# Attention followed by two gated layers on one core: later slots for three weights' conversions, the softmax epsilon on ScalarE, four buffers for P

## The chip, the core and the metric

One core of a Trainium2 chip. The metric is device time of the kernel in microseconds (us), as the median of three executions. One further execution was profiled. Its trace gives every instruction's engine, start and duration, and all rows below come from it. Engines: PE is TensorE, DVE is VectorE, ACT is ScalarE, POOL is GpSimd, and SP issues the transfers.

## The reference

Only the structure matters here. All weights come as 64-bit floats and everything is computed in 32 bits.

```python
scores = q @ k.T / 8 + (cum[:, None] - cum[None, :])   # 4 x 8 heads, 576 positions, causal
attn = np.exp(scores - np.max(scores, axis=-1, keepdims=True))
attn = attn / (np.sum(attn, axis=-1, keepdims=True) + 1e-09)
x = attn @ v                                            # -> 2304 x 512
h = x @ w_in                                            # 512 -> 2048
x = (h * np.tanh(softplus(h))) @ w_out                  # 2048 -> 512
out = (((x @ w1) * (x @ w2)) @ w3) @ wo2                # 512 -> 1024 -> 1024 -> 512
```

## The kernel before

The program has two phases. The second is a long run of matmuls for the two gated layers (lines 889, 908 and 928) that read converted weights. The first holds the attention and everything that prepares the second.

**Attention.** Heads are taken in 16 pairs, each pair in nine units (four row blocks per head and one block for the remaining 64 rows of both), so there are 144 units. A unit u goes through `scores` on PE (lines 391, 392, 401) into one of two PSUM tiles `ps_s`; `softmax_a` on DVE (lines 415 to 418), which writes the masked scores into the buffer `P[u % 3]` and finds their extreme, followed by an exponential on ACT (line 419) in place; `transposes` on PE (line 455) from P into one of two PSUM tiles `ps_t`; and `pt_parts`, which takes the transposed block out of `ps_t` as a high part on ACT (line 483) and a low part on DVE (line 485). After a head's units, `pv` multiplies by V (line 503). The row sums of a pair are finished by `inv_sums` (lines 426 and 427, 128x9 values), transposed (line 434), written to memory and read back as a broadcast tile R (lines 437 to 444); `x_rows` (515, 516) and `x_parts` (521, 88, 102) then make the pair's rows of x.

**What fills PE.** Between the units PE runs matmuls that have no hurry: the products of w3 and wo2 (line 550), and from batch to batch the first gated layer's `x @ w_in` (line 580), 12 matmuls to a tile, whose results go to memory through line 587 and 588. These need x of the four pairs of one batch, all of them for every tile: the last three of the 12 need the batch's last pair.

**Conversions.** A 64-bit weight block is loaded by SP (line 111, two buffers), scaled by POOL for the keys u (w_out) and v (w1 and w2) (line 124, two halves) or by ACT for the others (line 126), completed by three DVE instructions (lines 134, 135, 136, two output buffers), and for u and v stored by SP (line 143). There are 32 such jobs u0 to u15 and v0 to v15.

**What sets the order.** `phase_a` writes the code slot by slot: a table puts job i of the 32 at slot `W_OUT_SLOT + int(W_OUT_STEP * i)`. The code's order gives each instruction a priority. The build's scheduler then picks, from the instructions whose inputs and buffers it takes to be free, the one that comes first, so that an instruction written late can still stand early on its engine. The order that results is fixed in the program; at run time each engine takes its instructions strictly in that order, and a waiting one holds up all behind it.

Of the kernel before, what the change touches and what calls it, by code (L numbers as in the profile page):

```python
# [8 lines left out]
F32 = mybir.dt.float32  # L9
# [3 lines left out]
AF = mybir.ActivationFunctionType  # L13
ALU = mybir.AluOpType
# [4 lines left out]
B, H, S, D = 4, 8, 576, 64  # L19
# [24 lines left out]
MID = 7  # L44
EARLY = 10
W3_STEP = 2.25
W_OUT_STEP = 2.25
PRE = 6
WP_END = 51
W_IN_SLOT = 34  # L50
W_IN_STEP = 1.25
W_OUT_SLOT = 62
L1_S = (42, 75, 114, 153)

MM_PAIRS = ((0, 0), (0, 1), (1, 0))
# [12 lines left out]
class Kernel:  # L68
# [116 lines left out]
    def att_pool(self):  # L185
        nc = self.nc
        self.attp = self.tc.tile_pool(name="att", bufs=1)
        a = self.att = self.attp.__enter__()
        self.psp = self.tc.tile_pool(name="psa", bufs=1, space=PSUM)
        p = self.psp.__enter__()  # L190
        self.ps_s = [p.tile([128, 512], F32, name=f"ps_s{i}") for i in range(2)]
        self.ps_t = [p.tile([128, 512], F32, name=f"ps_t{i}") for i in range(2)]
        self.ps_v = p.tile([128, 1024], F32, name="ps_v")
        self.ident = a.tile([128, 128], F32, name="ident")
        self.m1 = a.tile([128, 512], BF16, name="m1")
        self.m4 = a.tile([128, TB], BF16, name="m4")
        self.pt = a.tile([128, 6 * PT_N + 3 * 64], F32R, name="pt")
        self.pt4 = self.pt[:, 6 * PT_N:]
        self.TT = [a.tile([128, 2, 1216], F32R, name=f"T{i}") for i in range(3)]
        self.T = [(t[:, 0], t[:, 1]) for t in self.TT]  # L200
        self.P = [a.tile([128, n], F32, name=f"P{i}") for i, n in enumerate((512, 512, S))]


    def decay_log(self):
# [67 lines left out]
    def zeros(self):  # L272

        nc = self.nc
        z = self.m1[:, :384]
        nc.gpsimd.memset(self.P[2][0:4], 1.0)
        for i in (0, 2, 1):
# [8 lines left out]
            for c in (d0, d0 + S):  # L286
                nc.scalar.copy(t2[0:4, c:c + S], self.P[2][0:4])

# [115 lines left out]
    def softmax_a(self, u):  # L404
        _, _, c = self.unit(u)
        nc = self.nc
        n = S if c == 4 else 128 * (c + 1)
        P = self.P[u % 3]
        i = (0, 1, 2, 3, 5, 6, 7, 8, 4)[u % 9]
        if u % 9 == 0:  # L410
            self.sums = self.att.tile([128, 16], F32, name=f"sum{u // 9}", tag="sum", bufs=2)
        st = self.sums[:, 9 + u % 3:10 + u % 3]
        ttr = nc.vector.tensor_tensor_reduce
        if c < 4:
            ttr(P[:, :n], self.ps_s[u % 9 % 2][:, :n], self.m1[:, 512 - n:], -0.125, 3.0e38, ALU.add, ALU.min, st)  # L415
        else:
            ttr(P[:, :TB], self.ps_s[0][:, :TB], self.m1[:, :TB], -0.125, 3.0e38, ALU.add, ALU.min, self.sums[:, 12:13])
            ttr(P[:, TB:n], self.ps_s[1][:, :TB], self.m4, -0.125, self.sums[:, 12:13], ALU.add, ALU.min, st)
        nc.scalar.activation(P[:, :n], P[:, :n], AF.Exp, bias=st, scale=-1.0,  # L419
                             accum_out=self.sums[:, i:i + 1])  # L420

    def inv_sums(self):

        nc = self.nc
        r = self.sums[:, 0:9]
        nc.vector.tensor_scalar(r, r, 1e-9, None, ALU.add)
        nc.vector.reciprocal(r, r)
        self.inv = r

# [18 lines left out]

    def transposes(self, u):
        _, _, c = self.unit(u)  # L450
        P = self.P[u % 3]
        for kc in range(c + 1):
            o = 128 * (kc % 4)
            k = 64 if kc == 4 else 128
            self.nc.tensor.transpose(self.t_bank(u, kc)[0:k, o:o + 128], P[:, 128 * kc:128 * kc + k], self.ident)  # L455
# [190 lines left out]
    def phase_a(self):  # L646
# [48 lines left out]
        def job(s, key, src, fin, *a):  # L695
            at(s, self.cv_load, key, src)
            conv.setdefault(s + 1, []).append(key)
            at(s + 2, fin, *a)
# [7 lines left out]
        for i in range(32):  # L706
# [3 lines left out]
            else:  # L710
                key, src, dst = f"v{f}", self.cols((self.w1, self.w2)[f % 2], f // 2), self.w12_scr
            job(W_OUT_SLOT + int(W_OUT_STEP * i), key, src, self.cv_store, key, dst[f])
        for p in range(NPAIR):
# [329 lines left out]
```

## Time and profile before

| what | value |
|---|---|
| median of three executions | 1089.82 us (1088.87 to 1092.64) |
| profiled execution | 1095.71 us |
| its span, from the first instruction to the last | 1094.0 us |
| PE busy | 980.8 us (90%) |
| DVE, ACT, POOL busy | 788.5, 639.1, 592.7 us |
| mean granted PE clock | 0.954 |

Busy time counts an instruction from start to end, also at a lower clock. The granted clock is told as a share of 2.4 GHz, so that 0.50 is the lower level, 1.2 GHz. The profiled execution's own time is 1.71 us over its span and 5.89 us over the median.

### The profile page before, as it was taken

The page shows a single profiled execution, that of the slowest core. Times are in us where ns is not written, and L with a number is a line of the kernel's source. Part 1 is how long each engine was busy: PE and PEld are TensorE (multiplying, and loading weights), DVE is VectorE, ACT ScalarE, POOL GpSimd, SP SyncE. Part 2 cuts the span into 40 slices and gives each one's busy share as a digit, 9 for nine tenths or more (in the row PEclk, how much of TensorE's full clock was granted, in tenths as well). Part 3 has the DMA queues.
Part 4 walks back from the last instruction along what each step waited for, and adds up shares of the span by engine and source line. Part 5 has one row for each costly group of instructions (what it writes and reads, how often), then busy time and mean ns, then how long its engine had stood idle before and what let it go on. Part 6 is the DMA issues. An engine that isn't in the chain of part 4 may idle for free. (4 is left out here: it accounts for less than half of the span.)

```text
span 1094.0 us, 20534 instructions
## 1 busy us (share of the span) xinstructions
PE 980.8 (90%) x6784; PEld 935.2 (85%) x6784; DVE 788.5 (72%) x1800; ACT 639.1 (58%) x1660; POOL 592.7 (54%) x690
## 2 busy tenths in 40 slices
PE   0797778888789888998979999999999999999998
PEld 0576657788789878998878999999999999999998
DVE  7977788785666776643897886868868687886821
ACT  7676778876665677764666454545545454454511
POOL 5956677775666677623685453534545353453500
PEclk9898869899889998998999999999999999999999
DMA  7865457667667867425864111121111112111100
GB/s 212 207 209 173 131 164 219 195 183 222 199 201 229 249 203 219 150 72 170 298 188 126 39 44 45 44 61 39 50 45 44 50 44 61 39 50 40 27 23 22
DMA packets 107086, 136.37 MB, mean 125 GB/s; under 512 B 11092, under 2 KB 83172, under 8 KB 106980
## 3 DMA queue, kind: packets, MB, share of 16 engines
q1 hardware_dynamic: 106980, 135.07, 41.7%
q8 instruction: 53, 0.87, 0.3%
q14 instruction: 53, 0.43, 0.1%
HBM read 98.39 MB, written 36.54 MB: 123 GB/s over the span
## 5 line engine op out<-in xcount | busy, mean ns | idle before, releaser
L580 PE MATMUL ps_l<-x,wi 128*128 128x288 f32 x1536 | 250.6, 312 | 14.5 <-ACT x L88 4.1
L580 PEld LDWEIGHTS ps_l<-x,wi 128*128 128x128 f32 x1536 | 224.7, 198 | 20.5 <-ACT hst L587 5.2
L889 PE MATMUL ps_x<-g,wo 128*128 128x288 f32 x1536 | 224.5, 297 | 6.8 <-POOL g L102 3.7
L889 PEld LDWEIGHTS ps_x<-g,wo 128*128 128x128 f32 x1536 | 209.6, 189 | 11.0 <-POOL g L102 6.0
L102 POOL TENSOR_TENSOR g<-mb,g 128x288 fp32r<-128x288 f32 x128 | 111.5, 871 | 135.5 <-ACT g L88 130.7
L102 POOL TENSOR_TENSOR T<-raw,T 64x288 fp32r<-64x288 f32 x128 | 113.3, 904 | 16.9 <-ACT T L339 11.9
L88 ACT CAST g<-mb 128x288 fp32r<-128x288 f32 x128 | 55.3, 432 | 112.8 <-DVE mb L853 82.5
L830 ACT ACTIVATE ma<-ma 128x288 f32<-128x288 f32 x128 | 56.6, 442 | 101.9 <-DVE ma L826 101.9
L908 PE MATMUL ps_y<-x,w 128*128 128x288 f32 x768 | 108.2, 296 | 2.6 <-ACT x L897 1.3
L908 PE MATMUL ps_l<-x,w 128*128 128x288 f32 x768 | 108.1, 295 | 0.0
L908 PEld LDWEIGHTS ps_y<-x,w 128*128 128x128 f32 x768 | 104.0, 189 | 3.0 <-ACT x L897 1.5
L908 PEld LDWEIGHTS ps_l<-x,w 128*128 128x128 f32 x768 | 104.3, 189 | 0.0
L455 PE MATMUL ps_t<-ident,P 128*128 128x128 f32 (+1 forms) x400 | 73.0, 301 | 32.9 <-DVE pt L485 32.5
L419 ACT ACTIVATE P<-P,sum 128x512 f32<-128x512 f32 (+2 forms) x144 | 85.4, 595 | 27.8 <-DVE sum L415 24.9
L485 DVE TENSOR_TENSOR pt<-ps_t,pt 128x128 fp32r<-128x128 f32 (+2 forms) x288 | 83.2, 331 | 24.6 <-ACT pt L483 24.1
L834 DVE SCALAR_TENSOR_TENSOR mb<-ma 128x288 f32<-128x288 f32 x128 | 63.3, 494 | 51.0 <-POOL g L102 49.2
L849 POOL TENSOR_TENSOR mb<-mb,hl 128x288 f32<-128x288 f32 x64 | 63.4, 991 | 62.7 <-DVE cs L847 29.3
L849 POOL TENSOR_TENSOR mb<-mb,hsp 128x288 f32<-128x288 f32 x64 | 61.8, 965 | 64.1 <-issue 25.7
L483 ACT CAST pt<-ps_t 128x128 fp32r<-128x128 f32 (+2 forms) x288 | 73.0, 314 | 34.5 <-PE ps_t L455 32.6
L848 DVE SCALAR_TENSOR_TENSOR ma<-cs,ma 128x288 f32<-128x288 f32 x128 | 89.5, 699 | 2.4
L455 PEld LDWEIGHTS ps_t<-ident,P 128*128 128x128 f32 (+1 forms) x400 | 52.3, 152 | 41.9 <-DVE pt L485 34.0
L847 DVE SCALAR_TENSOR_TENSOR cs<-mb,ma 128x288 f32<-128x288 f32 x128 | 73.6, 575 | 13.4 <-ACT ma L839 12.6
(123 smaller groups left out, 1917.7 us busy)
## 6 DMA issues: line engine op xcount, KB each, us to landing
raw<-in_qk_dram SPq DMA_DIRECT2D x64, 288.0 KB
h_scr<-h SPq DMA_DIRECT2D x96, 144.0 KB
hl<-h_scr SPq DMA_DIRECT2D x64, 144.0 KB
hsp<-h_scr SPq DMA_DIRECT2D x64, 144.0 KB
cvrt<-in_w3t_dram SPq DMA_DIRECT2D x16, 512.0 KB
cvri<-in_w_in_dram SPq DMA_DIRECT2D x16, 512.0 KB
cvru<-in_w_out_dram SPq DMA_DIRECT2D x16, 512.0 KB
cvrv<-in_w_dram SPq DMA_DIRECT2D x16, 512.0 KB
```

The source lines that it names most:

```text
L102: self.nc.gpsimd.tensor_tensor(lo[..., c], raw[..., c], f32(hi[..., c]), ALU.subtract)
L419: nc.scalar.activation(P[:, :n], P[:, :n], AF.Exp, bias=st, scale=-1.0, accum_out=self.sums[:, i:i + 1])
L455: self.nc.tensor.transpose(self.t_bank(u, kc)[0:k, o:o + 128], P[:, 128 * kc:128 * kc + k], self.ident)
L483: nc.scalar.copy(hi, a)
L485: nc.vector.tensor_tensor(self.pt_dst(hd, 1, k, 128 * c, w), a, f32(hi), ALU.subtract)
L580: mm(o[:, :TB], w, x, start=i == 0, stop=i == 11)
L834: self.nc.vector.scalar_tensor_tensor(b, a, 2.0, a, ALU.add, ALU.mult)
L847: nc.vector.scalar_tensor_tensor(e, b, 2.0, a, ALU.add, ALU.mult)
L848: nc.vector.scalar_tensor_tensor(a, e, 2.0, a, ALU.subtract, ALU.mult)
L849: nc.gpsimd.tensor_tensor(b, b, self.hl[c], ALU.mult)
L889: mm(self.xb(e), self.wo[f][:, 512 * a + 128 * e:512 * a + 128 * e + 128], g[:, TB * b:TB * b + TB], start=f == 0 and k == 0, stop=f == 15 ...
L908: mm(ps, self.w12[f, i][:, 512 * a + 128 * e:512 * a + 128 * e + 128], self.x2[e][:, TB * b:TB * b + TB], start=n == 0, stop=n == 11)
```

## The change

The 32 conversion jobs are written at slots 88 to 148 where they were at 62 to 134, in steps of 1.9 where it was 2.25. The buffer P has four tiles of 576 columns where it had three (of 512, 512 and 576), chosen by u % 4. The addition of 1e-9 to the nine sums of a pair is an ACT instruction; the reciprocal behind it stays on DVE.

```diff
-W_OUT_STEP = 2.25
+W_OUT_STEP = 1.9
...
-W_OUT_SLOT = 62
+W_OUT_SLOT = 88
...
-        self.P = [a.tile([128, n], F32, name=f"P{i}") for i, n in enumerate((512, 512, S))]
+        self.P = [a.tile([128, S], F32, name=f"P{i}") for i in range(4)]
...
-        P = self.P[u % 3]
+        P = self.P[u % 4]
...
-        nc.vector.tensor_scalar(r, r, 1e-9, None, ALU.add)
+        nc.scalar.activation(r, r, AF.Copy, bias=1e-9)
...
-        P = self.P[u % 3]
+        P = self.P[u % 4]
```

Three places of the instruction order show what this does. In all rows a number behind an underscore is the tile's place in the program; the number before it belongs to the name.

**DVE where the first w_out job stands.** Here cvu0 is that job's tile and sum6 the row sums of pair 6, whose second head's units these are. Before:

```order
L415 ISA P2_94,sum6_2058<-ps_s1_81,m1_86 128x256
L415 ISA sum6_2058 128x1
L415 ISA P1_93,sum6_2058<-ps_s0_80,m1_86 128x128
L415 ISA sum6_2058 128x1
L485 TENSOR_TENSOR pt_88<-ps_t1_83,pt_88 128x2x128
L485 TENSOR_TENSOR pt_88<-ps_t1_83,pt_88 128x128
L485 TENSOR_TENSOR pt_88<-ps_t0_82,pt_88 128x2x128
L134 TENSOR_SCALAR cvu0_2375<-cvu0_2375 128x512
L135 SCALAR_TENSOR_TENSOR cvu0_2375<-cvru0_2353,cvu0_2375 128x512
L516 TENSOR_TENSOR xx10_2187<-ps_v_84,xx10_2187 64x576
L136 SCALAR_TENSOR_TENSOR cvu0_2375<-cvru0_2353,cvu0_2375 128x512
```

After:

```order
L415 ISA P2_94,sum6_2059<-ps_s0_80,m1_86 128x128
L415 ISA sum6_2059 128x1
L134 TENSOR_SCALAR cvi15_2018<-cvi15_2018 128x512
L485 TENSOR_TENSOR pt_88<-ps_t0_82,pt_88 64x64 x2
L485 TENSOR_TENSOR pt_88<-ps_t1_83,pt_88 128x128
L135 SCALAR_TENSOR_TENSOR cvi15_2018<-cvri15_1982,cvi15_2018 128x512
L136 SCALAR_TENSOR_TENSOR cvi15_2018<-cvri15_1982,cvi15_2018 128x512
L134 TENSOR_SCALAR cvu0_3266<-cvu0_3266 128x512
L135 SCALAR_TENSOR_TENSOR cvu0_3266<-cvru0_3234,cvu0_3266 128x512
L415 ISA P0_92,sum6_2059<-ps_s0_80,m1_86 128x384
L415 ISA sum6_2059 128x1
L136 SCALAR_TENSOR_TENSOR cvu0_3266<-cvru0_3234,cvu0_3266 128x512
```

The job that the table moved from slot 62 to slot 88 stands among the same units of pair 6 as before. With each of the 32 jobs placed by how many units DVE has begun ahead of it, the first moves from 59 to 58 and the last (v15) from 129 to 130, and none moves by more than five.

**PE where the second batch of line 580 begins.** x4 to x7 are the x rows of pairs 4 to 7, T0 to T2 the operands of the scores. Before:

```order
L580 MATMUL ps_l0_64<-x5_0_2254,wi1_1374 128x288 x3
L580 MATMUL ps_l0_64<-x6_0_2594,wi1_1374 128x288 x3
L391 MATMUL ps_s1_81<-T2_91 128x256
L392 MATMUL ps_s1_81<-T2_91 128x256
L455 MATMUL ps_t0_82<-ident_85,P1_93 128x128 x2
L455 MATMUL ps_t1_83<-ident_85,P2_94 128x128 x3
...
L392 MATMUL ps_s1_81<-T1_90 128x256
L391 MATMUL ps_s0_80<-T1_90 128x384
L392 MATMUL ps_s0_80<-T1_90 128x384
L580 MATMUL ps_l1_65<-x7_0_2938,wi0_1343 128x288
L580 MATMUL ps_l0_64<-x7_0_2938,wi1_1374 128x288
```

After:

```order
L580 MATMUL ps_l0_64<-x5_0_2255,wi1_1375 128x288 x3
L580 MATMUL ps_l0_64<-x6_0_2566,wi1_1375 128x288 x3
L503 MATMUL ps_v_84<-pt_88,V7_2623 128x320
L503 MATMUL ps_v_84<-pt_88,V7_2623 128x192 x2
L455 MATMUL ps_t1_83<-ident_85,P0_92 128x128
L391 MATMUL ps_s0_80<-T2_91 128x256
...
L392 MATMUL ps_s0_80<-T1_90 128x384
L391 MATMUL ps_s1_81<-T1_90 128x512
L392 MATMUL ps_s1_81<-T1_90 128x512
L580 MATMUL ps_l1_65<-x7_0_2874,wi0_1344 128x288
L580 MATMUL ps_l0_64<-x7_0_2874,wi1_1375 128x288
```

In both, the batch begins with six groups on x4, x5 and x6 and then stops until x7 is made. Between the two pieces PE holds attention alone. That stretch takes in the scores of seven units in the old order (with two matmuls of line 580 up to the next group of them) and of eleven in the new one (with six). At the start of the third batch the same stretch has eight units before (with six such matmuls) and nine after (with 15).

**PE and SP at the end of the attention.** V15 is the last pair's V, x8 to x11 are the third batch, x12 to x15 the fourth, h2 the third batch's results, inv15 and R15 the last pair's sums. PE before and after:

```order
L580 MATMUL ps_l0_64<-x14_1_5250,wi0_1343 128x288 x3
L503 MATMUL ps_v_84<-pt_88,V15_5296 128x256 x2
L503 MATMUL ps_v_84<-pt_88,V15_5296 128x128 x2
L503 MATMUL ps_v_84<-pt_88,V15_5296 128x320 x6
L503 MATMUL ps_v_84<-pt_88,V15_5296 128x192 x2
L503 MATMUL ps_v_84<-pt_88,V15_5296 128x64
L580 MATMUL ps_l1_65<-x15_0_5487,wi0_1343 128x288
L580 MATMUL ps_l0_64<-x15_1_5491,wi0_1343 128x288
L580 MATMUL ps_l1_65<-x15_0_5487,wi0_1343 128x288 x2
```

```order
L503 MATMUL ps_v_84<-pt_88,V15_5269 128x320 x6
L503 MATMUL ps_v_84<-pt_88,V15_5269 128x192 x2
L503 MATMUL ps_v_84<-pt_88,V15_5269 128x64
L580 MATMUL ps_l1_65<-x8_1_3182,wi14_2032 128x288 x3
L580 MATMUL ps_l1_65<-x9_1_3523,wi14_2032 128x288 x3
L580 MATMUL ps_l1_65<-x10_1_3866,wi14_2032 128x288 x3
L580 MATMUL ps_l1_65<-x11_1_4214,wi14_2032 128x288 x3
L580 MATMUL ps_l0_64<-x8_1_3182,wi15_2075 128x288 x3
L580 MATMUL ps_l0_64<-x9_1_3523,wi15_2075 128x288 x3
L580 MATMUL ps_l0_64<-x10_1_3866,wi15_2075 128x288 x3
L580 MATMUL ps_l0_64<-x11_1_4214,wi15_2075 128x288 x3
L580 MATMUL ps_l1_65<-x12_0_4543,wi0_1344 128x288 x3
```

SP before and after:

```order
L588 DMA h_scr_66<-h2_13_1_5525 128x288
L588 DMA h_scr_66<-h2_14_1_5540 128x288
L588 DMA h_scr_66<-h2_15_1_5555 128x288
L437 DMA inv_scr_70<-inv15_5368 9x128
L442 DMA R15_5406<-inv_scr_70 64x576
L443 DMA R15_5406<-inv_scr_70 64x512
L444 DMA R15_5406<-inv_scr_70 64x64
L800 DMA vr0_5593<-w12_scr_68 128x512
```

```order
L588 DMA h_scr_66<-h2_10_1_5458 128x288
L437 DMA inv_scr_70<-inv15_5350 9x128
L588 DMA h_scr_66<-h2_11_1_5496 128x288
L442 DMA R15_5399<-inv_scr_70 64x576
L443 DMA R15_5399<-inv_scr_70 64x512
L444 DMA R15_5399<-inv_scr_70 64x64
L588 DMA h_scr_66<-h2_12_1_5511 128x288
L588 DMA h_scr_66<-h2_13_1_5526 128x288
```

Before, the last product with V stood behind the whole third batch and behind matmuls of the fourth, right ahead of the first that needs x15. Now 24 matmuls of the third batch and nine of the fourth stand between them. R15's loads, which stood behind all stores of h2, now stand ahead of four of them. From the last product with V to the first matmul of line 889 there were 78 matmuls of line 580, and there are 108.

## Rows read from the trace of the kernel before

**Rows 1.** Busy time by stretch: start:end, length, busy us (instructions) of each engine, clock, DMA share

```profile
33.50:211.20 177.70, 144.44 (x758) 119.58 (x759) 144.08 (x342) 136.46 (x353) 127.63 (x149) 0.88 0.63 179
211.20:434.40 223.20, 192.32 (x1302) 181.15 (x1300) 152.80 (x420) 148.34 (x430) 152.97 (x181) 0.92 0.71 212
434.40:501.40 67.00, 67.00 (x509) 65.92 (x507) 35.23 (x113) 44.78 (x136) 26.33 (x33) 1.00 0.35 112
600.00:1094.00 494.00, 487.55 (x3644) 484.29 (x3644) 355.71 (x774) 228.38 (x564) 200.20 (x222) 1.00 0.15 43
```

**Rows 2.** Waits of PE, 33.5 to 505 us: total us, times, longest us

```profile
PE ps_t L455 <- DVE pt L485: 32.5, 19, 4.0
PE ps_s L391 <- DVE sum L417: 6.2, 7, 3.5
```

**Rows 3.** Waits of DVE in the same stretch

```profile
DVE P L415 <- PE ps_t L455: 22.2, 26, 3.0
...
DVE cvu L134 <- POOL cvu L124: 19.8, 9, 6.4
DVE cvv L134 <- POOL cvv L124: 12.7, 6, 3.8
...
DVE P L417 <- PE ps_t L455: 9.9, 8, 2.7
```

**Rows 4.** PE in order of time, 260 to 304 us: start, us, [idle before <-releaser]

```profile
270.60 1.11 PE L455 MATMUL ps_t<-ident,P 128*128 128x128 f32 x4 [3.74 <-DVE pt L485]
...
282.44 2.01 PE L580 MATMUL ps_l<-x,wi 128*128 128x288 f32 x13
...
293.53 0.50 PE L580 MATMUL ps_l<-x,wi 128*128 128x288 f32 x2
297.72 1.12 PE L455 MATMUL ps_t<-ident,P 128*128 128x128 f32 x4 [3.69 <-DVE pt L485]
...
302.26 1.33 PE L580 MATMUL ps_l<-x,wi 128*128 128x288 f32 x4
```

**Rows 5.** Busy time in that stretch and in one at the lower clock

```profile
147.20:167.70 20.50, 15.48 (x56) 12.42 (x57) 16.92 (x47) 16.22 (x45) 14.47 (x18) 0.50 0.52 141
284.52:302.26 17.74, 11.93 (x65) 8.95 (x64) 14.87 (x42) 13.78 (x39) 11.56 (x14) 0.86 0.54 171
```

**Rows 6.** PE in order of time, 499 to 521 us

```profile
499.58 1.86 PE L503 MATMUL ps_v<-pt,V 128*128 128x256 f32 x13
505.20 0.40 PE L580 MATMUL ps_l<-x,wi 128*128 128x288 f32 x1 [3.75 <-ACT x L88]
505.95 8.85 PE L580 MATMUL ps_l<-x,wi 128*128 128x288 f32 x41 [0.35 <-ACT x L88]
...
519.90 0.69 PE L889 MATMUL ps_x<-g,wo 128*128 128x288 f32 x4
```

**Rows 7.** All engines in order of time, 499 to 504 us

```profile
502.14 0.75 DVE L516 TENSOR_TENSOR xx<-ps_v,xx 64x576 f32<-64x576 f32 x1 [2.62 <-ACT xx L515]
...
503.89 0.79 POOL L521 TENSOR_TENSOR xx<-xx,R 128x288 f32<-128x288 f32 x1 [16.73 <-DMA R<-inv_scr]
```

**Rows 8.** Busy time behind that wait

```profile
505.20:515.00 9.80, 9.25 (x42) 8.46 (x42) 2.44 (x5) 4.86 (x12) 4.62 (x7) 0.65 0.65 175
```

**Rows 9.** The chain that ended last, one of its pieces in the second phase

```profile
864.85 3.17 PE ps_l L908 x24
```

**Rows 10.** DVE and POOL in order of time around 269 us

```profile
269.21 1.01 DVE L134 TENSOR_SCALAR cvu<-cvu 128x512 int32<-128x512 int32 x1 [1.57 <-POOL cvu L124]
```

**Rows 11.** Lines 426 and 436: ns min/median/max, first and last start

```profile
L426 DVE TENSOR_SCALAR sum<-sum x16: 173/728/820, 59.2 to 488.9; 128x9 f32<-128x9 f32 x16
L436 ACT COPY inv<-ps_t x16: 238/255/257, 74.4 to 498.8; 9x128 f32<-9x128 f32 x16
```

**Rows 12.** The conversions' tiles, the DVE's first step: ns, first and last start

```profile
L134 DVE TENSOR_SCALAR cvu<-cvu x16: 411/428/1017, 228.1 to 337.1; 128x512 int32<-128x512 int32 x16
L134 DVE TENSOR_SCALAR cvv<-cvv x16: 414/428/1035, 340.7 to 449.0; 128x512 int32<-128x512 int32 x16
```

## The prediction, written before the changed kernel was run

> **What bounds the kernel now.** I read the busy time by stretch first. In the second phase, from 600 us on, PE is busy 487.55 of 494 us at full clock, and nothing in the change belongs to it; nor do the matmuls change in number. What can be won or lost lies ahead of it [rows 1]. From 33.5 to 434.4 us PE is idle 33.3 + 30.9 = 64.1 us and its granted clock is 0.88 and 0.92. From 434.4 to 501.4 us it is busy 67.00 of 67.00 us, with DVE at 35.23 and POOL at 26.33 us.
>
> The waits of PE come next. The largest is that of the transposes (line 455) for DVE's low parts (line 485), which free `ps_t`: 32.5 us; the scores wait 6.2 us for the masking of line 417 [rows 2]. So DVE is late, and I asked what DVE waits for: 22.2 + 9.9 = 32.1 us for transposes that free a P buffer, and 19.8 + 12.7 us, at a conversion, for POOL [rows 3]. One such case can be followed by hand: DVE waits 1.57 us for POOL at 269.21 us, then spends 1.01 us in line 134 [rows 10], and PE stands still for 3.74 us before the transposes of 270.60 [rows 4].
>
> The order of time shows where PE starves. From 284.45 to 302.26 us it has two matmuls of line 580, since x of the batch's last pair isn't made; a wait of 3.69 us lies in there [rows 4]. PE was busy 11.93 of 17.74 us, at a clock of 0.86 [rows 5].
>
> Last, the end of the attention. After the last product with V, which ends at 501.44, PE waits 3.75 and 0.35 us for x15 [rows 6]. Its rows were added up at 502.14 + 0.75 = 502.89 us, but POOL could multiply at 503.89 only, when R had landed [rows 7]. Behind the wait the clock is 0.65 for 9.8 us, with 9.25 us of PE work in it [rows 8].
>
> **The change part by part.** The sum is made against the span of 1094.0 us.
>
> *The later slots.* In the trace the conversions run on DVE from 228.1 to 449.0 us [rows 12]. The new order puts all 32 jobs among the same units within five, so the table's 26 slots are not carried out: the scheduler pulls the jobs forward to where their two buffers come free. I count no work moved into the free DVE time behind 434 us, and none taken out ahead of it: 0. What does change is who stands next to whom. The worst single case above was 3.74 us of PE, and a neighbour of that sort can be gained or lost: bounds -7.4 and +7.4, the two waits of [rows 4].
>
> *The stretch without line 580.* The same table lets PE take its matmuls earlier, so they run out earlier: eleven units instead of seven at the second batch, and about the same at the third. Against full clock the old seven lost 17.74 - 11.93 x 0.86 = 7.5 us [rows 5], 1.07 us each. Four more cost 4 x 1.07 = +4.3 us. Bounds: 0, if deeper buffering shortens each unit; +7.5, a whole further stretch of the old sort.
>
> *Four P buffers.* DVE may now mask unit u when unit u-4's transposes are done. The order uses part of that up again, since scores run further ahead too. Counted in the order, 123 units stood ahead of a transpose they had to wait for, with 1065 matmuls of lines 550 and 580 in between; now it is 107 units with 875 matmuls, 18% fewer. 18% of DVE's 32.1 us is 5.8 us [rows 3]. Half of it I put on PE's path, as DVE has slack of its own: -2.9 us, with bounds of -5.8 and 0.
>
> *The addition on ScalarE.* It takes 0.728 us on DVE in the median, sixteen times, 11.6 us [rows 11]. On ACT the nearest row is the copy of 9x128 at 0.255 us [rows 11], 4.1 us in all. PE waits for DVE in 38.7 us [rows 2] of the 467.9 us from 33.5 to 501.4, 8.3%, and that share of 11.6 us is -1.0 us. Bounds -11.6 and +4.1. The same instruction has taken as little as 0.173 us [rows 11]. The Trainium skill (SBUF — State Buffer, "Who interferes with whom") says that `tensor_scalar` on VectorE can need a port pair that it shares with GpSimd, and that whoever starts first keeps the other out for its whole instruction. By that rule most of the 0.728 us is a wait for GpSimd, which the next such instruction, line 134, would take over; only 16 x 0.173 = 2.8 us would be freed, and this term would be -0.2 us. The spread of line 134 from 411 to 1017 ns agrees with it [rows 12].
>
> *The end of the attention.* Between 501.44 and the first matmul of line 889 at 519.90 lie 18.46 us [rows 6], with 78 matmuls of line 580. At full clock 24 matmuls take 3.17 us [rows 9], so the 78 need 10.3 us and 8.2 us are lost. In the new order 33 matmuls (4.4 us) stand between the last V product and x15. The way from 501.44 to 505.20 took 3.76 us, 1.0 of them for R [rows 6, 7], whose loads are no longer behind the last stores. So the wait for x15 goes, and with it the low clock behind it. What is late next is line 889: its chain (loads, the gate on ACT and DVE) starts with x15 and took until 519.90, now 1.0 us less, 17.5 us, while PE has 108 matmuls or 14.3 us of work. A wait of 3.2 us is left where 8.2 us were lost: -5.0 us. Bounds: -8.2, if that chain starts earlier too; -1.8, if the clock falls again behind the new wait and costs another 3.2 us (9.25 x 0.35) [rows 8].
>
> Sum: 0 + 4.3 - 2.9 - 1.0 - 5.0 = -4.6 us. The span would be 1089.4 us and the profiled execution, 1.71 us over its span, 1091.1; the median of the runs stood 5.89 us under the old profiled one, which gives **1085.2 us**.
>
> **The rivals.**
>
> *Slower: the longer stretch drops to the lower clock and stays there.* From 147.20 to 167.70 us PE ran at 0.50 throughout, with transposes and scores and no large supply of other work, and lost 20.50 - 15.48 x 0.50 = 12.8 us, 62% [rows 5]. The stretch that I price above lost 42%. The twenty units at both batches, at 17.74 / 7 = 2.53 us each, last 51 us; a fifth more lost is +10.2 us. With the rest of the sum that is 1095.4 us. For it: the new stretch is half as long again. Against it: the old one began at full clock and fell only behind the wait of 3.69 us. It decides from about 16 of the 20 units at 0.50 (8 us). The Trainium skill (TensorE: Matmul & The Clock Gate, "HAM oscillation — how this bites in real kernels") tells of kernels that pay for the lower clock again after each wait; this trace does so behind the waits of 270.6 and 505.2.
>
> *No change.* The losses of the starved stretch eat the gain at the end, -5.0 + 4.3, and the waits on P only move over to `ps_t`, whose two banks are as before: 1089 us. For it: PE's largest wait [rows 2] is for `ps_t`, not for P.
>
> *The change does what the table says.* The jobs leave the starved stretch: the two waits of 3.74 and 3.69 us go [rows 4], and they fill DVE where PE is at 67.00 of 67.00 us [rows 1]. 1085.2 - 7.4 = 1077.8 us. The order speaks against it.
>
> *More gain than counted.* The wait at line 889 goes too (-3.2) and P gives its 5.8 us (-2.9): 1079 us. For it: 64.1 us of idle time, much of it at DVE's waits.
>
> **How the numbers follow.** Differences under 0.3%, 3.3 us, can't be told from no change here. Forecast 0.36; no change 0.20; slower 0.24; more gain 0.15; as the table says 0.05. The forecast's own range is 1082 to 1088: three quarters of it are faster than 1086.5. Faster 0.27 + 0.15 + 0.05 = 0.47; same 0.09 + 0.20 = 0.29; slower 0.24. The range must take in most of the gain cases and of the slower one: 1077 to 1096 us.
>
> **What would show it.** Right: conversions on DVE from about 228 to 449 us again; no wait of PE for x15, and one of 2 to 4 us at the first line 889; a starved stretch near 275 to 305 us with eleven units; DVE's waits for P near 26 us. Wrong: the clock at 0.50 through that stretch, conversions behind 455 us, or a larger wait for `ps_t` than 32.5 us.

## The result and the profile of the changed kernel

| | median of six executions | lowest to highest | ratio to before, 95% interval |
|---|---|---|---|
| before | 1089.69 us | 1088.87 to 1094.80 | |
| changed | 1099.53 us | 1094.98 to 1100.87 | 1.0077 [1.0055, 1.0099] |

The three executions of above are among the six of before. The change makes the kernel 0.8% slower: 8 us by the ratio and 10 by the medians are lost where 4.6 us were to be won, and 1099.53 us stand against a forecast of 1085.2 in a range of 1077 to 1096. A trap lies in the two profiles: the profiled execution of the changed kernel, 1094.98 us (span 1093.2), is the fastest of its six, while that of before, 1095.71 us, stands 5.9 us over the median of its kernel. The two spans differ by 0.8 us, and hide the loss. So I argue times from medians, and use the traces for what stands where and what waits.

The busy time of the changed kernel by the stretches of [rows 1] (start:end, length, PE, PEld, DVE, ACT, POOL, clock, DMA share, GB/s):

```profile
33.50:211.20 177.70, 143.58 (x706) 117.70 (x707) 133.79 (x332) 132.12 (x347) 122.77 (x143) 0.82 0.62 176
211.20:434.40 223.20, 194.33 (x1309) 180.56 (x1308) 156.44 (x422) 155.40 (x446) 158.69 (x186) 0.92 0.72 213
434.40:501.40 67.00, 66.73 (x510) 65.85 (x509) 33.58 (x108) 44.75 (x139) 27.77 (x35) 1.00 0.37 119
600.00:1093.00 493.00, 487.25 (x3644) 484.18 (x3644) 354.96 (x774) 228.45 (x564) 200.49 (x222) 1.00 0.16 43
```

The second phase is as before. The first stretch isn't: PE is as long busy, but at 0.82 instead of 0.88, and in the same time it gets 706 matmul records done instead of 758.

Its waits from 33.5 to 505 us, beside [rows 2, 3] (us in total, times, longest):

```profile
PE ps_s L391 <- DVE sum L415: 16.4, 16, 4.2
PE ps_t L455 <- DVE pt L485: 15.1, 13, 2.7
...
DVE P L415 <- PE ps_t L455: 23.4, 27, 2.5
DVE P L417 <- PE ps_t L455: 2.5, 2, 1.6
```

PE's wait for `ps_t` has halved, from 32.5 us, and a wait of the scores for the masking of line 415 has taken its place. DVE's waits for a P buffer fell from 32.1 to 25.9 us.

The conversions and the addition (ns min/median/max, first and last start):

```profile
L134 DVE TENSOR_SCALAR cvu<-cvu x16: 410/544/1020, 228.3 to 326.4; 128x512 int32<-128x512 int32 x16
L134 DVE TENSOR_SCALAR cvv<-cvv x16: 407/427/1015, 340.4 to 449.5; 128x512 int32<-128x512 int32 x16
L426 ACT ACTIVATE sum<-sum x16: 195/201/247, 59.8 to 486.3; 128x9 f32<-128x9 f32 x16
```

A table that names slots 26 later leaves the conversions where [rows 12] have them. The addition takes 201 ns on ACT.

The end of the attention, PE and then POOL in order of time, beside [rows 6, 7]:

```profile
499.91 1.76 PE L503 MATMUL ps_v<-pt,V 128*128 128x256 f32 x13
501.51 6.60 PE L580 MATMUL ps_l<-x,wi 128*128 128x288 f32 x48
508.32 3.48 PE L580 MATMUL ps_l<-x,wi 128*128 128x288 f32 x24 [0.22 <-ACT hst L587]
515.43 6.59 PE L580 MATMUL ps_l<-x,wi 128*128 128x288 f32 x36 [3.63 <-ACT hst L587]
521.86 0.69 PE L889 MATMUL ps_x<-g,wo 128*128 128x288 f32 x4
...
503.26 1.56 POOL L521 TENSOR_TENSOR xx<-xx,R 128x288 f32<-128x288 f32 x2 [15.16 <-DVE xx L516]
```

PE no longer waits for x15. But it waits 3.63 us at 515.43 for the copies of line 587, and the first line 889 comes at 521.86 instead of 519.90.

### The profile page after: what moved, and what is told of

The parts are those of the page before. It is cut to its first block, busy times and chain, and to the rows that moved or that the text cites. A ratio compares the mean times of both kernels' runs of the same rounds, so it can differ in the third digit from the quotient of the medians.

```text
span 1093.2 us, 20423 instructions
## 1 busy us (share of the span) xinstructions
PE 983.4 (90%) x6784; PEld 934.4 (85%) x6784; DVE 778.7 (71%) x1784; ACT 641.6 (59%) x1676; POOL 596.4 (55%) x690
## 5 line engine op out<-in xcount | busy, mean ns | idle before, releaser
L580 PE MATMUL ps_l<-x,wi 128*128 128x288 f32 x1536 | 243.3, 307 | 12.1 <-ACT hst L587 9.5
L580 PEld LDWEIGHTS ps_l<-x,wi 128*128 128x128 f32 x1536 | 218.5, 195 | 17.5 <-ACT hst L587 12.2
L485 DVE TENSOR_TENSOR pt<-ps_t,pt 128x256 fp32r<-128x256 f32 (+2 forms) x288 | 84.2, 332 | 37.7 <-ACT pt L483 37.0
L483 ACT CAST pt<-ps_t 128x256 fp32r<-128x256 f32 (+2 forms) x288 | 74.3, 312 | 45.7 <-PE ps_t L455 37.9
L419 ACT ACTIVATE P<-P,sum 128x128 f32<-128x128 f32 (+4 forms) x144 | 84.9, 591 | 15.2 <-DVE sum L415 13.8
L455 PE MATMUL ps_t<-ident,P 128*128 128x128 f32 (+1 forms) x400 | 76.8, 305 | 16.5 <-DVE pt L485 15.1
L415 DVE CUSTOM_DVE_ANT_0 P<-ps_s,m 128x128 f32<-128x128 f32 (+3 forms) x128 | 61.5, 483 | 38.3 <-PE ps_t L455 23.4
L391 PE MATMUL ps_s<-T 128*128 128x256 f32 (+2 forms) x128 | 51.9, 410 | 39.9 <-POOL T L102 16.8
```

The lines of the kernel that those rows point to most:

```text
L483: nc.scalar.copy(hi, a)
L485: nc.vector.tensor_tensor(self.pt_dst(hd, 1, k, 128 * c, w), a, f32(hi), ALU.subtract)
L580: mm(o[:, :TB], w, x, start=i == 0, stop=i == 11)
```

## The experiments

One table holds all of them. "x15" is the start of the last line 521, by which the last pair's x is about to be done, in the profiled execution; "rest" is the span less that; "580" counts the matmuls of line 580 from 33.5 to 205 us; "clock" is the granted clock from 33.5 to 500 us. (Without the addition these lines are 520 and 579.) Ratios compare with executions of the kernel before on the same chip; x15 and the counts come from one execution each. Those of "before" and "changed" stood 5.9 us over and 4.6 us under their medians, so their x15 times can't be set against each other; "changed, again" was profiled 0.3 us under its median.

| kernel | ratio [95%] | x15 us | rest us | 580 | clock |
|---|---|---|---|---|---|
| before | 1 | 504.6 | 589.4 | 133 | 0.91 |
| changed | 1.0077 [1.0055, 1.0099] | 504.0 | 589.2 | 80 | 0.89 |
| changed, again | 1.0079 [1.0059, 1.0100] | 507.2 | 590.2 | 77 | 0.90 |
| buffers | 1.0070 [1.0042, 1.0098] | 514.2 | 587.0 | 96 | 0.89 |
| addition | 1.0087 [1.0065, 1.0109] | 511.8 | 589.5 | 84 | 0.89 |
| slots | 0.9940 [0.9917, 0.9963] | 491.7 | 586.4 | 142 | 0.92 |
| slots and buffers | 1.0111 [1.0089, 1.0134] | 511.7 | 587.4 | 103 | 0.90 |
| slots and addition | 1.0082 [1.0061, 1.0104] | 506.7 | 589.3 | 88 | 0.91 |
| buffers and addition | 1.0129 [1.0106, 1.0152] | 518.9 | 588.6 | 76 | 0.89 |
| no addition at all | 1.0075 [1.0052, 1.0098] | 511.8 | 587.9 | 108 | 0.91 |
| slot 75, step 2.25 | 0.9995 [0.9978, 1.0013] | 502.1 | 588.6 | 120 | 0.90 |
| slot 96, step 1.6 | 1.0011 [0.9995, 1.0028] | 502.7 | 586.9 | 129 | 0.91 |
| extra matmuls, before | 1.0149 [1.0130, 1.0168] | 516.9 | 588.4 | 120 | 0.96 |
| extra matmuls, slots | 1.0176 [1.0159, 1.0192] | 525.7 | 587.1 | 118 | 0.93 |
| buffers, order of before | 0.9983 [0.9965, 1.0001] | 503.3 | 588.7 | 123 | 0.91 |
| addition, order of before | 1.0014 [0.9997, 1.0032] | 503.4 | 588.7 | 120 | 0.90 |
| both, order of before | 1.0001 [0.9985, 1.0017] | 500.1 | 588.9 | 120 | 0.92 |
| no edit, order of "addition" | 1.0078 [1.0054, 1.0103] | 506.8 | 590.6 | 84 | 0.91 |
| order of the changed kernel, addition on VectorE | 1.0060 [1.0038, 1.0083] | 503.0 | 589.1 | 84 | 0.91 |
| all three, order of "slots" | 0.9913 [0.9889, 0.9936] | 498.2 | 586.7 | 108 | 0.91 |

**Where.** In all twenty traces the rest is 586.4 to 590.6 us, while x15 moves from 491.7 to 525.7. So a kernel is slow or fast by when the last pair's x comes. How much work of line 580 an order leaves for behind it is another matter; the part on the end of the attention comes back to it.

**Each edit alone, and the change again.** The edits are the three hunks of the diff, one at a time.

> Only the four P buffers. At equal PE work the changed kernel is 3.7 us late at 180 us and 6.5 us late at 496 us, and this kernel's PE order equals the changed one's up to the 36th unit. Theory (the buffers let the scheduler pull scores ahead and PE starves earlier): 3 to 8 us slower than before, late by 3 us at 180 us already. Rival (the later conversion slots cost the time): within 2 us of before.

> Only the later slots and the step of 1.9. The order equals that of before up to about the 72nd unit. Theory of the buffers: within 3 us of before. Rival (the slots cost): 6 to 10 us slower, all of it lost behind 275 us. As the table reads (conversions out of the starved stretch): 5 us faster.

> Only the addition on ScalarE. By the sum of the prediction 1 us faster. If any edit that makes the scheduler deal anew costs time, whatever it is: 2 to 6 us slower, late from about 130 us on, where the order first has more starved units.

> The changed kernel as it is, for a trace of a usual execution: the profiled one was the fastest of six. If the usual ones lose more in the attention, it is 9 to 12 us late at 496 us and wins the same 7 us behind it; if they lose at the hand-over to the second phase, it is 6 to 7 us late at 496 us and wins nothing from there to 600 us.

Two edits that shorten or take away waits each cost as much as the whole change; the third, which moves no conversion (225.6 to 440.2 us on DVE), gains. The loss of the change was there again. Of the expectations, that for the buffers was met; the addition cost 9.5 us where 2 to 6 were the most expected, and the slots gained 6.5 us where the theory had at most 3. That is nearest to what the table reads like, 5 us, but the conversions that were to move for it didn't.

**Two at a time, and the addition left out.** If the edits cost by themselves, their ratios should add up, and less work should not be slower. The last of the four leaves out the 1e-9:

```diff
-        nc.vector.tensor_scalar(r, r, 1e-9, None, ALU.add)
```

> Later slots and four buffers, the addition on DVE. Alone the one gave a ratio of 0.994 and the other 1.007. If the two effects add: 1.001, about 1092 us. If the slots' gain belongs to one order of the instructions, which the buffers deal anew: like the buffers alone, 1.005 to 1.009.

> Later slots and the addition on ScalarE, three buffers. Alone 0.994 and 1.0087. If effects add: 1.003, about 1094 us. If the order decides: like the addition alone, 1.006 to 1.011.

> Four buffers and the addition on ScalarE, the old slots. If effects add: 1.0157, about 1108 us. If each only makes the scheduler deal another order from the same pack: 1.005 to 1.010, like each alone.

> The kernel before without the addition of 1e-9 (left out of the computation), so that it has sixteen instructions less and none more. If the addition on ScalarE cost time by itself (its queue, its hop to DVE): 0.5 to 3 us faster than before. If the cost came from the new order that any change of a duration makes: its time can lie to either side, and 3 to 9 us slower with less work would show it.

They don't add up: 0.9940 and 1.0070 make 1.0111, and sixteen instructions less make 1.0075. Two of the four, 1.0111 and 1.0129, lie outside both ranges given for them. Nothing that was taken out can cost 8 us. This is where a theory of costs of the single edits fell for me, and what they have in common remained: after each the scheduler sets up the order of every engine anew.

**Other slots.** The table alone, with other numbers.

```diff
-W_OUT_SLOT = 62
+W_OUT_SLOT = 75
```
```diff
-W_OUT_STEP = 2.25
-W_OUT_SLOT = 62
+W_OUT_STEP = 1.6
+W_OUT_SLOT = 96
```

> The kernel before with the first conversion's slot at 75 instead of 62 and the step unchanged (the other two edits are absent). Theory of the dealt order (any edit of the table or of an operation deals every engine's order anew, and the time follows from how many microseconds TensorE then works at the lower clock before the last pair's x): no fixed sign; between 0.993 and 1.012 of the time before, that is 1083 to 1103 us, and the end minus the time at which the last pair's x is done again 585 to 590 us. Rival, a later slot is what makes it faster (slots 88 with step 1.9 gave 0.994): about half of that gain, 0.996 to 0.998, some 1088 us.

> The kernel before with the first conversion at slot 96 and a step of 1.6 (the other two edits absent). Theory of the dealt order: no fixed sign, 0.993 to 1.012 of the time before; end minus the last pair's x 585 to 590 us; its place in that range goes with the microseconds at half clock before the last x (72 in the fastest run so far, 106 in the slowest). Rival, a later slot is what makes it faster: at least as fast as slots 88 with step 1.9, 0.990 to 0.995, some 1082 us.

"A later slot is faster" is out: 88 gains 0.6%, 75 and 96 nothing. Such an edit changes no instruction, only where each stands, so these differences are those of the order itself.

**Extra matmuls against the lower clock.** The first stretch was slower at a lower clock, so the clock could be the lever.

```diff
+            if s in range(22, 48) or s in range(70, 88) or s in range(106, 124):
+                for _ in range(6):
+                    self.nc.tensor.matmul(self.ps_v[:, 0:256], self.m1[:, 0:128], self.m1[:, 0:256], start=True, stop=True)
```

> The kernel before with 372 extra bf16 matmuls of 256 columns on a constant, into columns of a PSUM tile that nothing reads, six in each of the slots 22 to 47, 70 to 87 and 106 to 123, so that TensorE has work where it otherwise waits. They change no output. At the duration that other matmuls of 256 columns have (about 0.107 us at full clock, twice that at half) they are some 40 to 60 us of extra work on TensorE. Theory, the lower clock costs the time: half-clock time before the last x falls from 82 us to under 60, the last x comes within 5 us of 505 or earlier, and the time is 0.99 to 1.005 of that before although work was added. Rival, the idle time is what costs and the clock only goes with it: the extra work fills waits in part and delays the rest, the last x comes 15 to 40 us later, 1.014 to 1.037 of the time before.

> The kernel with the later slots alone (0.994) and the same 372 extra matmuls in the same slots. It had 72 us at half clock before the last x. Theory, the lower clock costs the time: half-clock time falls under 55 us and the time stays within 0.988 to 1.0 of that before. Rival, the idle time costs and the clock goes with it: 1.008 to 1.03.

The kernel before with the extra matmuls, busy time from 33.5 to 500 us:

```profile
33.50:500.00 466.50, 411.03 (x2795) 369.92 (x2796) 332.18 (x863) 324.86 (x897) 309.19 (x362) 0.96 0.63 183
```

Before, PE was busy 402.36 us at 0.91 there. A mean of 0.91 is (1 - 0.91) / 0.5 = 18% of 466.5 us, or 84 us, at the lower level; 0.96 is 37 us. So the clock rose as the theory said, and x15 came 12.3 us later all the same. In the kernel with later slots it hardly rose, from 0.92 to 0.93, and the ratio went from 0.9940 to 1.0176. What my theory forecast, a time of 1.005 at most, failed: where the clock was lifted, the time grew.

Why it grew these two runs don't show, since they add more than work. The scheduler dealt a new order here as well: with the extra ones left out, PE's matmuls stand in another order than before from the 316th on, and an order alone was worth up to 1.3% in other runs. And the extra matmuls (line 747) wait for line 516, which reads other columns of the same PSUM tile:

```profile
PE ps_v L747 <- DVE xx L516: 5.3, 5, 3.0
```

No run added them with the order held, so whether a higher clock alone would win time stays open. That it doesn't decide the time another row shows: "no addition at all" has the clock of before, 0.91, and is 0.75% slower. The Trainium skill (Perfetto Trace Analysis, "Optimization Strategies") gives as the general goal a matmul engine as highly utilized as possible; here 8.7 us more of busy time at a higher clock came with 1.5% more time.

**The order held.** Six kernels whose order is fixed. Edges in the scheduler alone chain the instructions of each engine in the order that another kernel got; no instruction is added. Where the addition stands on another engine than in the kernel whose order is taken, the scheduler places that one instruction. In the traces all 6784 matmuls on PE, and all instructions on DVE, ACT and POOL but the additions, stand in the order that was taken.

```diff
+def pin(nc, tc):
+    traced = list(nc.cur_bb.bb.instructions)
+    for e, code in ORDER.items():
...
+        for a, b in zip(place, place[1:]):
+            tc.add_manual_dep(mine[b], mine[a].name, mybir.DependencyInfo(mybir.DependencyClass.NoSync, mybir.DependencyReason.DATA), reason="pin")
...
         tile_forgetting_attention_moe(tc, *args)
+        pin(nc, tc)
```

> The four P buffers with every engine's instructions held in the order of the kernel before (edges in the scheduler alone, no instruction added). Theory, the order that the scheduler deals is what costs, not the fourth buffer: the loss of the four-buffer kernel (1.007) is gone, and since a buffer more can only end waits when the order stays, 0.994 to 1.001 of the time before, with TensorE's half-clock time before the last x near the 82 us of before. Rival, the four buffers themselves cost (larger tiles, other addresses, scores that come earlier and disturb other engines): 1.005 to 1.010 again.

> The addition on ScalarE with every other instruction held in the order of the kernel before. Theory of the dealt order: 0.997 to 1.002, the addition itself is worth the 1.0 us of the prediction or nothing. Rival, the place of the addition costs (it stands behind other work of ScalarE, the reciprocal and with it R and x come later): 1.006 to 1.011 again.

> The work of the kernel before, the addition on VectorE and three P buffers, with every other instruction held in the order that the kernel with only the addition on ScalarE got (1.0087). Theory of the dealt order: the loss stays, 1.005 to 1.012, although no operation differs from before. Rival, the operation's engine: 0.998 to 1.002.

> All three edits, with every instruction but the additions held in the order that the kernel with only the later slots got (0.994). Theory of the dealt order: 0.988 to 0.996, where the scheduler's own order for the same three edits gave 1.008. Rival, the buffers or the addition cost by themselves, whatever the order: 1.003 to 1.012.

> Four P buffers and the addition on ScalarE, with all else held in the order of the kernel before; the scheduler's own order for these two edits gave 1.0129. Theory of the dealt order: the loss is gone, 0.996 to 1.002 (the two alone, so held, gave 0.9983 and 1.0014). Rival, the two edits cost when they come together: 1.006 to 1.014.

> The changed kernel's order, with the addition back on VectorE (placed by the scheduler, all else held); four P buffers and the later table remain, since that order needs them. Theory of the dealt order: the loss of the changed kernel (1.008) stays, 1.005 to 1.012, and the time by which TensorE is behind the kernel before grows between 180 and 205 us, as in the changed kernel. Rival, the addition's engine: 0.996 to 1.002.

Each of the six came out in the range that the theory of the order gave, and outside that of its rival. The same two edits cost 1.3% in the order they were dealt and nothing in the order of before. Since the table of slots sets nothing but an order, "both, order of before", 1.0001, has every instruction of the changed kernel, 1.0077, and only the order differs. Before's work in another order costs 0.8%. All three edits, in the order that the later slots alone were dealt, take 1082.97 us, 0.9% less than before and the fastest of all; how much of that is beyond the slots alone (0.9940) the intervals don't tell.

With the order held, each edit shows what it does by itself. One wait of the kernel before, then waits with four buffers, then with the addition on ACT, both in the order of before:

```profile
DVE pt L485 <- ACT pt L483: 24.1, 30, 2.4
```
```profile
DVE pt L485 <- ACT pt L483: 36.2, 38, 2.9
PE ps_t L455 <- DVE pt L485: 32.6, 20, 4.0
...
DVE P L415 <- PE ps_t L455: 14.6, 12, 3.6
```
```profile
DVE sum L427 <- ACT sum L426: 10.5, 6, 6.4
```

With four buffers DVE's waits for a P buffer behind line 455 fall from 32.1 to 14.6 us, against 25.9 in the changed kernel's order. But DVE's wait for the high parts on ACT (line 483) grows from 24.1 to 36.2 us, and PE's wait for `ps_t` stays at 32.6 us, where it was 32.5: the waiting moves on and doesn't leave PE's path. The addition on ACT makes DVE's reciprocal wait 10.5 us, for a ratio that can't be told from 1.

**What differs in a slow order.** PE of the changed kernel in order of time, as the first batch's last pair gets its x:

```profile
178.66 1.46 PE L580 MATMUL ps_l<-x,wi 128*128 128x288 f32 x9
...
181.60 0.53 PE L580 MATMUL ps_l<-x,wi 128*128 128x288 f32 x2 [0.68 <-ACT x L88]
182.33 0.66 PE L455 MATMUL ps_t<-ident,P 128*128 128x128 f32 x4 [0.20 <-DVE pt L485]
183.41 0.66 PE L455 MATMUL ps_t<-ident,P 128*128 128x128 f32 x4 [0.42 <-ACT P L419]
185.95 0.58 PE L391 MATMUL ps_s<-T 128*128 128x256 f32 x1 [1.88 <-POOL T L102]
...
187.15 0.58 PE L391 MATMUL ps_s<-T 128*128 128x256 f32 x1 [0.40 <-POOL T L102]
...
187.91 1.33 PE L580 MATMUL ps_l<-x,wi 128*128 128x288 f32 x4
...
191.22 1.96 PE L580 MATMUL ps_l<-x,wi 128*128 128x288 f32 x10
```

The same place with both edits in the order of before:

```profile
179.44 1.59 PE L580 MATMUL ps_l<-x,wi 128*128 128x288 f32 x10 [0.74 <-DVE wp L92]
181.96 0.80 PE L580 MATMUL ps_l<-x,wi 128*128 128x288 f32 x4 [0.94 <-POOL x L102]
182.60 1.03 PE L455 MATMUL ps_t<-ident,P 128*128 128x128 f32 x8
...
183.94 3.37 PE L580 MATMUL ps_l<-x,wi 128*128 128x288 f32 x24
...
188.84 1.78 PE L580 MATMUL ps_l<-x,wi 128*128 128x288 f32 x12
...
190.48 1.17 PE L580 MATMUL ps_l<-x,wi 128*128 128x288 f32 x7
```

x is there at 181.6 and 182.0 us. In the order of before PE then has 24 matmuls of line 580 while the next units are made ready. In the changed order it has two, then units that wait for their T on POOL (1.88 us), and the batch's matmuls start in earnest at 191.22. The stretch around it in both (same columns as above):

```profile
143.00:191.30 48.30, 35.40 (x157) 28.25 (x156) 35.54 (x97) 39.52 (x104) 38.57 (x46) 0.69 0.61 172
```
```profile
143.00:191.30 48.30, 37.16 (x205) 32.04 (x204) 38.61 (x97) 40.24 (x108) 40.91 (x47) 0.82 0.63 180
```

In equal time the changed kernel does, by an estimate from busy time and mean clock, 35.40 x 0.69 = 24.4 us of work at full clock, the other 37.16 x 0.82 = 30.5 us. The column "580" marks the same in other orders. Of the kernels without extra matmuls, the seven with 120 or more of these matmuls by 205 us lie at 0.994 to 1.001. Of the ten others, with at most 108, nine lie at 1.006 to 1.013, and one, all three edits in the order of the slots, at 0.991 with 108.

But the block is not where the time stays lost. Counted further, with the scores of line 391 within four units of each other at each of these times, the changed kernel catches up and then falls behind again (matmuls of line 580 from 33.5 us to the time given):

| kernel | 205 us | 280 us | 313 us | 400 us | 496 us |
|---|---|---|---|---|---|
| order of before, three kernels | 120 to 123 | 384 to 398 | 444 to 460 | 786 | 1155 to 1170 |
| changed, two profiles | 80, 77 | 377, 372 | 408, 408 | 743, 726 | 1099, 1080 |

At 205 us it is 40 to 46 matmuls short, at 280 us 7 to 26, at 313 us, behind the stretch of the second batch, 36 to 52, and at 496 us 56 to 90. No run moved one place of an order alone: which places cost the 8 us stays open.

## Why the prediction was wrong, step by step

**The step that failed** is the part of the sum that lies ahead of the last product with V, "0 + 4.3 - 2.9 - 1.0", or +0.4 us. There the changed kernel fell 7 to 12 us behind: 56 to 90 matmuls of line 580 at 496 us, at the 3.17 / 24 us of [rows 9]. Less the 5.5 to 6.6 us that the end gave back, that is 1 to 6 us in these profiles where the medians say 8 to 10, and single executions don't tell it closer. The sum prices each edit as if the rest of the program stayed where it was, with a few places corrected for the new order. The order dealt after any edit is worth more than the edits: 0.9983 against 1.0070 for the buffers, 1.0014 against 1.0087 for the addition, 1.0001 against 1.0129 for both.

**The later slots, 0 with bounds of 7.4.** The conversions stayed, as predicted. The edit alone was worth 0.0060 x 1091 = -6.5 us, inside the bounds, by its order; which place of the order gave it isn't known, and the two other tables gave nothing.

**The stretch without line 580, +4.3.** At the second batch it was about right. Between the two full runs of line 580 the changed kernel has 28.66 us with six of its matmuls:

```profile
284.76:313.42 28.66, 21.24 (x113) 17.28 (x112) 20.77 (x62) 20.39 (x62) 21.38 (x25) 0.82 0.71 195
```

28.66 - 21.24 x 0.82 = 11.2 us lost. The 7.5 us of before end one group of line 580 earlier; to the same end before has

```profile
284.52:304.84 20.32, 14.51 (x78) 11.46 (x77) 16.51 (x49) 15.44 (x44) 14.04 (x18) 0.83 0.57 179
```

20.32 - 14.51 x 0.83 = 8.3 us, so 3 us are added where 4.3 were priced. A like stretch at the first batch, 143 to 191 us, I left out: 6.1 us less work done than in the order of before, though most of it was made up by 280 us. What comes after 313 us, another 19 to 42 matmuls short by 496 us, is in no term.

**Four P buffers, -2.9.** With the order held the edit gave 0.0017 x 1092 = -1.9 us, interval -3.8 to +0.1, which can't be told from 0. DVE's waits in the changed kernel, 25.9 us, are the 26 that were predicted, but that half of such a gain reaches PE isn't shown: with the order held 17.5 us of DVE's waits for P went, and PE's wait for `ps_t` stayed. As the price of what the scheduler makes of the edit the term has the wrong sign: +7.6 us.

**The addition, -1.0.** The duration was well judged (201 ns for 255), the time not: +1.5 us with the order held, not to be told from 0, and +9.5 as dealt. I counted what DVE is freed of, not that the reciprocal now waits for ACT.

**The end of the attention, -5.0.** This term came true in size, and in the main for the reason given. Matmuls of line 580 behind the last product with V, which ends at 501.44 us before and at 501.67 after (start:end, length, PE, PEld, clock, DMA share, GB/s):

```profile
501.44:620.00 118.56, 60.01 (x366) 55.39 (x366) 0.93 0.57 182
```
```profile
501.67:620.00 118.33, 61.03 (x408) 56.71 (x408) 0.97 0.57 184
```

The changed order leaves 42 more of them for behind it, 5.5 us of work at full clock, and from there to the end of the span it took 592.6 us before and 591.5 after; in the second profile of the changed kernel, where that product ends at 504.89 us, 592.5. So they fill waits that are there anyway, which makes 5.5 to 6.6 us. No run changed the end alone. "Rest" can't show this gain, since it lies in what PE no longer has to do ahead of x15, and the loss there was larger. The wait for x15 went, and so did the wait for R. The one left came elsewhere than predicted: not at line 889 but 3.63 us at 515.43, for the copies of line 587, and the first line 889 started 2.0 us later than before.

**The rivals.** The slower one named 1095.4 us, the right side by the right kind of thing, a longer stretch at a lower clock. But it put it at the second and third batch, and the stretch at the second ran at 0.82 rather than 0.50; the lowest clock, 0.69, was at the first, where the loss was mostly made up. The reason behind "no change", that the waits on P only move on, shows with the order held. "The change does what the table says" is out, as the conversions stayed. Of the signs, the conversions, the wait for x15, the starved stretch and the waits for P all came as named for a right forecast, and the kernel was slower: none of them looked at the rest of the order.

## What to carry to other kernels

Where a scheduler orders the program, each edit is two: its own cost, and a new order for every engine. Here the order was worth from -0.6% to +1.3%, and the two edits that are more than an order, by themselves, at most 0.4% by their intervals. Measure them apart: hold the order and make the edit, or keep the edit out and take the order; and before believing a small gain or loss, try neighbouring values of the same number. Find first the event after which hardly anything changes any more (here the last x, with 586 to 591 us behind it in every kernel), and price an edit by when that event comes, not by the waits that it removes. Count too how much work an order moves from ahead of that event to behind it.

## What the hardware showed that I had not expected

More work raised PE's clock from 0.91 to 0.96 between 33.5 and 500 us, and the kernel became 1.5% slower: a higher granted clock isn't by itself time won. How much of the loss is the added work, its waits or the new order isn't shown. And executions of one program differ by more than some edits are worth: the same program took 1088.87 to 1094.80 us in six executions, so that two profiles, each of one execution, showed 0.8 us where the medians differ by 9.8.
